# Mixing k and v of six attention pairs with tokens on the partitions

## Chip, cores, metric

One NeuronCore of a Trainium2 chip; the runs did not all use the same chip. The metric is device time in microseconds (us) of one execution. The kernel before takes 245.04 us (median of 6 runs, 244.96 to 245.6).

## The reference

Block-sparse attention whose k and v blocks are first mixed by an 8x8 matrix per head (made by five Sinkhorn steps), then a bilinear feed-forward network (FFN). Four batches, 8 heads, 768 tokens, 64 columns per head; the FFN is 512 to 1536 to 512.

```python
k_sorted = np.einsum('bhij,bhjcd->bhicd', P, k_b)      # block i = sum over blocks j
v_sorted = np.einsum('bhij,bhjcd->bhicd', P, v_b)
scores   = scale * np.matmul(q_b, k_sb.transpose(0, 1, 2, 4, 3))   # within a block of 96 tokens
attn     = softmax(scores)
x        = matmul(attn, v_sb)      # ... heads side by side: 3072 x 512
out      = ((x @ w_a) * (x @ w_b)) @ w_out
```

## The kernel before

Heads are worked in pairs; a batch has four (0 to 15 in all). While the TensorE (PE) runs the FFN of batch b, the attention of batch b+1 is slipped in between its steps as "units": `c_` (mix k and v), `s_` (scores), `o_` (attention output). Tokens are loaded so that partition p holds tokens 6p to 6p+5 (`NCH` = 6). The mix of a pair is 12 matmuls for k and 12 for v. Their stationary operand is a 128-token by 64-column piece of k or v, the moving one the 128x128 mixing matrix `s_all`; the result has head columns on the partitions, so k comes out transposed, as the scores need it, and v is turned back by a DMA transpose.

```python
    def stage_mix(g, what, engines):
        src2 = loaded[g][0 if what == "k" else 1]
        to = (kTs if what == "k" else vTs)[g % NBUF]
        pitch, whole = (BLK, S + PAD) if what == "k" else (P, NB * P)
        mix = psA.tile([P, 2, 512], FP32, tag="A", name="mix")
        for c in range(NCH):
            for e in range(2):
                nc.tensor.matmul(
                    mix[e * D:(e + 1) * D, c // 3, c % 3 * P:(c % 3 + 1) * P],
                    lhsT=src2[:, e, c * D:(c + 1) * D],
                    rhs=s_all[:, 2 * g + e], start=True, stop=True)
        for hf, eng in enumerate(engines):
            n = 2 // len(engines)
            for u in range(n):
                d1 = _ap(to, (hf + u) * 3 * CG, [[whole, P], [CG, 3], [pitch, NB], [1, CG]])
                s1 = _ap(mix, (hf + u) * 512, [[1024, P], [P, 3], [CG, NB], [1, CG]])
                copy(eng, d1, s1)
        if what == "v" and g > HP:
            nc.sync.dma_start_transpose(out=vss[g % NBUF][:, :, V0:V0 + P],
                                        in_=to.rearrange("p i t -> p (i t)"))
# ... cut ...
        def units_full(b):
            g0, us = b * HP, []

            def c_(g):
                if g < 2 * HP - 2:
                    turn_q(g)
                stage_mix(g, "k", ("act",))
                stage_mix(g, "v", ("dve", "act"))
                if 2 * HP - 2 <= g < B * HP - 2:
                    nc.gpsimd.tensor_copy(out=gate, in_=kTs[g % NBUF][0:1, 0:1])
                    load_pair((g + 2) // HP, (g + 2) % HP)

            def s_(g):
                stage_scores(g)
                if g == HP:
                    turn_v(g)
                if g in (HP, HP + 1):
                    stage_q(g + 2)
                if 2 * HP <= g + 1 < B * HP:
                    pair_q(g + 1)
                    stage_q(g + 1)

            def o_(g):
                stage_o(g)
                to_xT(g)

            for u, n in ((c_, 0), (s_, 0), (c_, 1), (s_, 1), (c_, 2), (o_, 0), (s_, 2), (c_, 3),
                         (o_, 1), (s_, 3), (o_, 2), (o_, 3)):
                us.append(lambda u=u, g=g0 + n: u(g))
            return us
# ... cut ...
        def paced(ab, po, units, spare):
            steps = ab + po
            total = len(steps) - 2 * spare
            done = 0
            for now, step in enumerate(steps, 1):
                step()
                while done < len(units) and done * total < now * len(units):
                    units[done]()
                    done += 1
```

An FFN step `ffn_ab` is 8 matmuls with 128x128 weights and 384 moving columns; an output half-step is 6 with 512 columns. Output tiles `o_sb` have three buffers, `hT` has two.

The softmax here doesn't subtract the row's maximum and nothing guards it: scores larger than these inputs give would overflow.

## Time and profile before

| Kernel before | Value | View |
|---|---|---|
| Time | 245.04 us; profiled span 243.3 us | runs, page |
| PE busy | 237.4 us, 98% | page, part 1 |
| Batch 1, batch 2: first FFN matmul to that of the next batch | 54.52 us each, PE busy throughout | windows |
| Batch 3 (no attention inside) to its last matmul | 46.8 us | windows |
| One pair's mix on PE, pauses included | 0.89 us | timeline, worked out below |

The busy table and the slices of the page (40 equal slices of the span, tenths busy; "PEclk" is the granted clock; PE is the TensorE, PEld its weight loads, DVE the VectorE, ACT the ScalarE, POOL the GpSimd, SP the queue of the SyncE):

```profile
PE 237.4 (98%) x2309; PEld 141.6 (58%) x2309; DVE 109.1 (45%) x258; ACT 104.4 (43%) x204; POOL 61.4 (25%) x88
...
PE   7999999999999999999999999999999999999994
...
PEclk9999999999999999999999999999999999999999
DMA  5999999985999589993964369923524310000132
```

PE is the bound from the second slice to the last; the rest has slack. The stages in the windows view (first column start and end, then length, busy us and number of instructions of each engine, granted clock, DMA share, GB/s). The borders come from the chain of work that ended last; they lie 0.17 us behind the first FFN matmul's start in the timeline, in each stage alike, so the lengths are the same:

```profile
84.17:138.69 54.52, 54.52 (x490) 31.41 (x489) 23.57 (x47) 23.89 (x47) 12.67 (x20) 1.00 0.80 124
138.69:193.21 54.52, 54.52 (x490) 31.41 (x489) 23.59 (x47) 23.89 (x47) 7.16 (x11) 1.00 0.54 97
193.21:240.01 46.80, 46.77 (x276) 26.40 (x274) 15.37 (x27) 13.73 (x28) 0.00 (x0) 1.00 0.09 34
```

The Trainium skill, "Perfetto Trace Analysis", section "Tensor Engine Instruction (MATMUL, LD_WEIGHTS)", says that the end of a matmul is estimated by the profiler, not observed, and this trace agrees: a 384-column matmul lasts 326 ns although they start 162.5 ns apart. A pause shorter than that overlap leaves no idle time. So read starts. One mix in batch 1, in the PE timeline (start us, us to the modelled end of the group, group):

```profile
100.55 0.81 PE L332 MATMUL pf<-xT,w_b_sb 128*128 128x384 bf16 x4
101.30 0.53 PE L281 MATMUL mix<-s_all,k 128*64 128x128 bf16 x12
101.66 0.50 PE L281 MATMUL mix<-s_all,v 128*64 128x128 bf16 x12
102.09 0.82 PE L332 MATMUL pf<-xT,w_a_sb 128*128 128x384 bf16 x4
```

The fourth FFN matmul starts at 100.55 + 3 x 0.1625 = 101.04, so its successor could start at 101.20. The first mix matmul starts at 101.30, and the next FFN matmul at 102.09: the mix takes 102.09 - 101.20 = 0.89 us of PE. The weight loads (PEld) of the same stretch show the entry:

```profile
100.39 0.58 PEld L332 LDWEIGHTS <-w_b_sb 128*128 128x128 bf16 x4
101.30 0.36 PEld L281 LDWEIGHTS <-k 128*64 128x64 bf16 x12 [0.32 <-issue]
101.60 0.39 PEld L281 LDWEIGHTS <-v 128*64 128x64 bf16 x12
102.09 0.44 PEld L332 LDWEIGHTS <-w_a_sb 128*128 128x128 bf16 x4
```

A FFN weight load starts while the matmul ahead of it runs (100.39 before 100.55). The first 64-column load does not: it starts with its matmul, at 101.30. ("[0.32 <-issue]" says that the engine stood idle for 0.32 us just before, for nothing that the profile shows.)

### The profile page before, as it was taken

Reading aid. Unit: us, or ns where it says so; the run is one execution under the profiler, and the core shown is the slowest. Engines: PE = TensorE matmul, PEld = TensorE weight load, DVE = VectorE, ACT = ScalarE, POOL = GpSimd, SP = SyncE. Lnnn points to the kernel's source line nnn. Section 1 sums busy time; section 2 is a strip of 40 time slices with the busy share of each in tenths; the row PEclk is TensorE's granted clock in tenths of the full one; section 3 lists DMA queues with packets and bytes.
Section 4 is the critical chain, followed back from the end, with each engine's and each line's share of the span. In section 5 each row is a group of like instructions: output and inputs, shape, how many; then the busy total and the mean of one; then the engine's idle time right before and its main releaser. Section 6 shows DMA issues by size and latency. Waiting matters only on the chain.

```text
span 243.3 us, 5625 instructions
## 1 busy us (share of the span) xinstructions
PE 237.4 (98%) x2309; PEld 141.6 (58%) x2309; DVE 109.1 (45%) x258; ACT 104.4 (43%) x204; POOL 61.4 (25%) x88
## 2 busy tenths in 40 slices
PE   7999999999999999999999999999999999999994
PEld 7776666666554466666654466666654466665442
DVE  6774557555435234464534144363625144344110
ACT  3675853565630175736330165737330133333001
POOL 8766569623220053240400054200000000000000
PEclk9999999999999999999999999999999999999999
DMA  5999999985999589993964369923524310000132
GB/s 78 202 198 196 196 201 201 203 138 83 158 204 153 130 70 155 171 138 70 136 115 122 115 120 114 159 51 58 47 75 131 109 43 0 3 0 1 46 129 86
DMA packets 53930, 28.04 MB, mean 115 GB/s; under 512 B 30736, under 2 KB 50960, under 8 KB 53904
## 3 DMA queue, kind: packets, MB, share of 16 engines
q0 software_dynamic: 20944, 14.16, 41.6%
q1 hardware_dynamic: 32816, 13.45, 28.0%
q8 instruction: 18, 0.29, 0.5%
q14 instruction: 8, 0.07, 0.1%
q10 hardware_dynamic: 144, 0.07, 0.1%
HBM read 28.32 MB, written 6.29 MB: 142 GB/s over the span
## 4 chain that ended last, share of the span: by engine, by line
PE 93%; DVE 4%; ACT 1%; DMA 1%; issue 0%
PE pf L332 52%; PE po L377 24%; PE mix L281 4%; PE o_ps L231 3%; PE sc L302 2%; PE mixh L180 2%; PE po L362 1%; PE vs_ps L208 1%; PE xt_ps L222 1%; PE sc L195 1%; DMA p_nat<-in_sort_net_dram 1%; PE heat L168 1%; PE two L332 1%; PE q_ps L260 1%; DVE xp L237 1%
## 5 line engine op out<-in xcount | busy, mean ns | idle before, releaser
L353 DVE TENSOR_TENSOR hT<-a_sb,pf 128x384 bf16<-128x384 bf16 x95 | 52.6, 553 | 73.8 <-PE pf L332 46.4
L332 PE MATMUL pf<-xT,w_a_sb 128*128 128x384 bf16 x380 | 78.0, 326 | 0.2 <-ACT xT L162 0.2
L332 PE MATMUL pf<-xT,w_b_sb 128*128 128x384 bf16 x380 | 77.5, 326 | 0.0
L352 ACT CAST a_sb<-pf 128x384 bf16<-128x384 f32 x95 | 45.5, 479 | 60.9 <-PE pf L332 41.3
L377 PE MATMUL po<-w_out_sb,hT 128*128 128x512 bf16 x276 | 61.9, 379 | 0.0
L332 PEld LDWEIGHTS <-w_b_sb 128*128 128x128 bf16 x384 | 37.5, 98 | 24.8 <-issue 0.3
L332 PEld LDWEIGHTS <-w_a_sb 128*128 128x128 bf16 x384 | 34.9, 98 | 22.2
L377 PEld LDWEIGHTS <-hT 128*128 128x128 bf16 x276 | 26.3, 98 | 30.0
L162 ACT COPY o_sb<-po 128x512 f32<-128x512 f32 (+1 forms) x13 | 7.5, 577 | 46.8 <-PE po L377 45.2
L164 DVE COPY o_sb<-po 128x512 f32<-128x512 f32 (+1 forms) x12 | 7.9, 656 | 35.2 <-PE po L377 26.3
L307 ACT ACTIVATE eT<-sc 96x768 bf16<-96x768 f32 x24 | 18.0, 802 | 6.9 <-PE sc L302 6.9
L542 POOL COPY gate<-kT 1x1 bf16<-1x1 bf16 x8 | 1.4, 179 | 74.7 <-ACT kT L162 74.7
L237 DVE TENSOR_TENSOR xp<-o_ps,rec 96x512 bf16<-96x512 f32 x24 | 15.9, 684 | 0.6 <-DVE rec L235 0.2
L162 ACT CAST kT<-mix 128x384 bf16<-128x384 f32 x24 | 10.3, 482 | 8.0 <-PE mix L281 8.0
L95 POOL DMA_DIRECT2D k<-in_k_dram x16 | 11.6, 724 | 4.5 <-PE pf L332 2.3
L95 POOL DMA_DIRECT2D v<-in_v_dram x16 | 11.5, 721 | 3.1 <-DMA w_b_sb<-in_moe_w_b_dram 1.2
L231 PEld LDWEIGHTS <-eT 96*128 96x128 bf16 x256 | 10.4, 97 | 3.2 <-DVE xp L237 0.6
L235 DVE RECIPROCAL rec<-o_ps 96x8 f32<-96x8 f32 x32 | 5.6, 189 | 13.8 <-PE o_ps L231 13.8
L231 PE MATMUL o_ps<-vs,eT 96*128 96x65 bf16 x256 | 11.3, 193 | 0.2 <-DVE xp L237 0.2
L246 POOL COPY qc<-q 128x768 bf16<-128x768 bf16 x10 | 8.4, 842 | 7.2 <-DMA q<-in_q_dram 7.2
L95 POOL DMA_DIRECT2D q<-in_q_dram x12 | 8.7, 721 | 1.7 <-DMA w_a_sb<-in_moe_w_a_dram 0.7
L168 PE MATMUL heat<-warm 128*128 128x128 bf16 x84 | 7.6, 264 | 1.3 <-DVE warm L77 1.3
(80 smaller groups left out, 158.3 us busy)
## 6 DMA issues: line engine op xcount, KB each, us to landing
out_dram<-o_sb SPq DMA_DIRECT2D x17, 256.0 KB, 2.0
k<-in_k_dram POOLq DMA_DIRECT2D x16, 192.0 KB, 6.0
v<-in_v_dram POOLq DMA_DIRECT2D x16, 192.0 KB, 6.4
q<-in_q_dram POOLq DMA_DIRECT2D x12, 192.0 KB, 6.7
w_a_sb<-in_moe_w_a_dram POOLq DMA_DIRECT2D x6, 256.0 KB, 9.8
w_b_sb<-in_moe_w_b_dram POOLq DMA_DIRECT2D x6, 256.0 KB, 10.0
w_out_sb<-in_moe_w_out_dram POOLq DMA_DIRECT2D x3, 512.0 KB, 10.8
out_dram<-o_sb SPq DMA_DIRECT2D x12, 128.0 KB, 2.4
```

The costliest lines, as they stand in the source:

```text
L95: nc.gpsimd.dma_start(out=to, in_=_ap(t, base, [[W, P], [S * D, 2], [1, W]]))
L162: nc.scalar.copy(out=out, in_=in_)
L168: nc.tensor.matmul(ps[:, 0:cols], lhsT=warm[:, 0:P], rhs=warm[:, 0:cols], start=True, stop=True)
L231: nc.tensor.matmul(o_ps[:, e, i * (D + 1):(i + 1) * (D + 1)], lhsT=eT[:, hf, e, i * BLK:i * BLK + P], rhs=vs[0:BLK, i0 + i, V0 - 1 + e * ( ...
L237: nc.vector.tensor_tensor(out=_ap(xp, i0 * 2 * D, [[nxp * 2 * D, BLK], [D, 2], [2 * D, NBH], [1, D]]), in0=_ap(o_ps, 1, [[1024, BLK], [511 ...
L246: nc.gpsimd.tensor_copy(out=qc.rearrange("p c e d -> p e c d"), in_=loaded[g][2].rearrange("p e (c d) -> p e c d", c=NCH))
L281: nc.tensor.matmul(mix[e * D:(e + 1) * D, c // 3, c % 3 * P:(c % 3 + 1) * P], lhsT=src2[:, e, c * D:(c + 1) * D], rhs=s_all[:, 2 * g + e], ...
L307: nc.scalar.activation(out=eT[:, hf, :, 0:HB], in_=sc[0:BLK, :, 0:HB], func=AF.Exp, scale=float(scale))
L332: nc.tensor.matmul(pf[:, 0:HW], lhsT=w_sb[:, kc, m * P:(m + 1) * P], rhs=x_cols(b, kc, t), start=(kc == 0), stop=(kc == KA - 1))
L352: nc.scalar.copy(out=a_sb, in_=pf[:, 0:HW])
L353: nc.vector.tensor_mul(out=hT[:, m, t * HW:(t + 1) * HW], in0=a_sb, in1=ab[1][:, 0:HW])
L377: nc.tensor.matmul(held["po"], lhsT=hTs[b][:, m, c * P:(c + 1) * P], rhs=w_out_sb[:, m, :], start=(m == 0), stop=(m == KO - 1))
```

## The change

For pairs 10 to 15 the operands of the mix trade places: `s_all` becomes the stationary operand and a whole head (128 x 384) the moving one, so that the result keeps tokens on the partitions. That makes 4 matmuls per pair out of 24, in the very form of the FFN's. The price is that k is no longer transposed: k and v go through a DMA transpose each, and POOL puts the columns in order (`in_order`), before v is turned back as ever. Since that takes longer, at least two other units stand between each of these mixes and its scores, and batch 2's first two mixes (pairs 12 and 13) are moved into batch 1's steps. The cut of the diff below holds one more move: for pairs 10 to 15 the copy and the DMA transpose of q, which `s_` of the pair before issued, are issued in `c_`, behind the transposes of k and v. Output tiles get six buffers, and `hT` gives one of its two back to make room.

```diff
                 d1 = _ap(to, (hf + u) * 3 * CG, [[whole, P], [CG, 3], [pitch, NB], [1, CG]])
                 s1 = _ap(mix, (hf + u) * 512, [[1024, P], [P, 3], [CG, NB], [1, CG]])
                 copy(eng, d1, s1)
-        if what == "v" and g > HP:
-            nc.sync.dma_start_transpose(out=vss[g % NBUF][:, :, V0:V0 + P],
-                                        in_=to.rearrange("p i t -> p (i t)"))
+
+    def plain(g):
+        return g >= 2 * HP + 2
+
+    def stage_plain(g, what, engines):
+        src2 = loaded[g][0 if what == "k" else 1]
+        mix = psA.tile([P, 2, 512], FP32, tag="A", name="mix")
+        for e in range(2):
+            nc.tensor.matmul(mix[:, e, 0:W], lhsT=s_all[:, 2 * g + e], rhs=src2[:, e],
+                             start=True, stop=True)
+        nat = att.tile([P, NCH, 2, D], BF16, tag="nat", name="nat")
+        step = 2 // len(engines)
+        for u, eng in enumerate(engines):
+            copy(eng, nat[:, :, u * step:(u + 1) * step].rearrange("p c e d -> p e c d"),
+                 mix[:, u * step:(u + 1) * step, 0:W].rearrange("p e (c d) -> p e c d", c=NCH))
+        turned = att.tile([P, NCH, P], BF16, tag="turned", name="turned")
+        nc.sync.dma_start_transpose(out=turned, in_=nat.rearrange("p c e d -> p (c e d)"))
+        st[g, what] = turned
+
+    def stage(g, what, engines):
+        (stage_plain if plain(g) else stage_mix)(g, what, engines)
+
+    def in_order(g, what):
+        if what == "k":
+            to = kTs[g % NBUF][:, 0:S].rearrange("p (i c t) -> p c i t", i=NB, c=NCH)
+        else:
+            to = vTs[g % NBUF][:, :, 0:BLK].rearrange("p i (c t) -> p c i t", c=NCH)
+        nc.gpsimd.tensor_copy(out=to, in_=st[g, what].rearrange("p c (i t) -> p c i t", i=NB))
+
+    def return_v(g):
+        nc.sync.dma_start_transpose(out=vss[g % NBUF][:, :, V0:V0 + P],
+                                    in_=vTs[g % NBUF].rearrange("p i t -> p (i t)"))
 
 
# ... cut: hT bufs=1, o_sb bufs=3 -> bufs=6 in both places ...
-            for u, n in ((c_, 0), (s_, 0), (c_, 1), (s_, 1), (c_, 2), (o_, 0), (s_, 2), (c_, 3),
-                         (o_, 1), (s_, 3), (o_, 2), (o_, 3)):
-                us.append(lambda u=u, g=g0 + n: u(g))
+        plan(0, "c4", "s4", "c5", "s5", "c6", "o4", "s6", "c7", "o5", "s7", "o6", "o7")
+        plan(1, "c8", "s8", "c9", "s9", "c10", "o8", "c11", "o9", "s10", "c12", "s11", "o10", "o11",
+             "c13")
+        plan(2, "s12", "c14", "s13", "o12", "c15", "s14", "o13", "s15", "o14", "o15")
+        after = [[] for _ in seq]
+        for n, (b, u, g) in enumerate(seq):
+            if u is c_ and plain(g):
+                late = 3 if g % HP == 0 else 2
+                after[n + 1] += [lambda g=g, what=what: in_order(g, what) for what in "kv"]
+                if late == 3:
+                    after[n + 3].append(lambda g=g: nc.gpsimd.tensor_copy(
+                        out=gate, in_=xT_of(g // HP - 1)[0:1, HP - 1, 0:1]))
+                after[n + 2 * late - 3].append(lambda g=g: load_later(g))
+                after[n + late].append(lambda g=g: return_v(g))
# ... cut: c_, s_, o_ around stage(); for plain pairs c_ calls pair_q and stage_q behind k and v, which s_ of
# the pair before did; paced() runs batch 1's last unit one step before its end ...
```

More of the change, by code (lines that the diff above doesn't have):

```diff
@@ L336, in hT_of @@
         if b not in hTs:
-            hTs[b] = ffp.tile([P, KO, S], BF16, tag="hT", name="hT")
+            hTs[b] = ffp.tile([P, KO, S], BF16, tag="hT", name="hT", bufs=1)
         return hTs[b]
@@ L363, in ffn_last @@
                                  rhs=w_out_sb[:, m, n0:n1], start=(m == 0), stop=(m == KO - 1))
-            o_sb = ffp.tile([P, 512], FP32, tag="o_sb", name="o_sb", bufs=3)
+            o_sb = ffp.tile([P, 512], FP32, tag="o_sb", name="o_sb", bufs=6)
             copy(eng, o_sb[:, 0:n1 - n0], po[:, 0:n1 - n0])
@@ L384, in store @@
     def store(b, c, po):
-        o_sb = ffp.tile([P, DMODEL], FP32, tag="o_sb", name="o_sb", bufs=3)
+        o_sb = ffp.tile([P, DMODEL], FP32, tag="o_sb", name="o_sb", bufs=6)
         copy("act" if c % 2 == 0 else "dve", o_sb, po)
@@ L531, in units_half, with c_ @@
             return us
-        def units_full(b):
-            g0, us = b * HP, []
-            def c_(g):
-                if g < 2 * HP - 2:
-                    turn_q(g)
-                stage_mix(g, "k", ("act",))
-                stage_mix(g, "v", ("dve", "act"))
-                if 2 * HP - 2 <= g < B * HP - 2:
-                    nc.gpsimd.tensor_copy(out=gate, in_=kTs[g % NBUF][0:1, 0:1])
-                    load_pair((g + 2) // HP, (g + 2) % HP)
-            def s_(g):
-                stage_scores(g)
-                if g == HP:
-                    turn_v(g)
-                if g in (HP, HP + 1):
-                    stage_q(g + 2)
-                if 2 * HP <= g + 1 < B * HP:
-                    pair_q(g + 1)
-                    stage_q(g + 1)
-            def o_(g):
-                stage_o(g)
-                to_xT(g)
-            for u, n in ((c_, 0), (s_, 0), (c_, 1), (s_, 1), (c_, 2), (o_, 0), (s_, 2), (c_, 3),
-                         (o_, 1), (s_, 3), (o_, 2), (o_, 3)):
-                us.append(lambda u=u, g=g0 + n: u(g))
-            return us
+        def c_(g):
+            if g < 2 * HP - 2:
+                turn_q(g)
+            stage(g, "k", ("act",))
+            stage(g, "v", ("dve", "act"))
+            if plain(g):
+                pair_q(g)
+                stage_q(g)
+            else:
+                if g > HP:
+                    return_v(g)
+                if g >= 2 * HP - 2:
+                    nc.gpsimd.tensor_copy(out=gate, in_=kTs[g % NBUF][0:1, 0:1])
+                    load_later(g)
@@ new lines, in s_, with o_, load_later, plan @@
+        def s_(g):
+            stage_scores(g)
+            if g == HP:
+                turn_v(g)
+            if g in (HP, HP + 1):
+                stage_q(g + 2)
+            if 2 * HP <= g + 1 < B * HP and not plain(g + 1):
+                pair_q(g + 1)
+                stage_q(g + 1)
+        def o_(g):
+            stage_o(g)
+            to_xT(g)
+        def load_later(g):
+            if g < B * HP - 2:
+                load_pair((g + 2) // HP, (g + 2) % HP)
+        seq = []
+        def plan(b, *names):
+            for name in names:
+                seq.append((b, {"c": c_, "s": s_, "o": o_}[name[0]], int(name[1:])))
@@ L564, in interleave, with unit @@
+        def unit(u, g, then):
+            u(g)
+            for f in then:
+                f()
+        units = [[] for _ in range(B)]
+        for (b, u, g), then in zip(seq, after):
+            units[b].append(lambda u=u, g=g, then=then: unit(u, g, then))
         def interleave(steps, units, spare, slow=0):
@@ L571, in interleave, with paced @@
                     done += 1
-        def paced(ab, po, units, spare):
+        def paced(ab, po, units, spare, last):
             steps = ab + po
             total = len(steps) - 2 * spare
-            done = 0
+            main, done = len(units) - last, 0
             for now, step in enumerate(steps, 1):
                 step()
-                while done < len(units) and done * total < now * len(units):
+                while done < main and done * total < now * main:
                     units[done]()
                     done += 1
+                if now == len(steps) - 1 and last:
+                    units[main]()
         steps = [lambda: ffn_ab(0, 0, 0, begun[0:2]), lambda: ffn_ab(0, 1, 0, begun[2:4]),
@@ L591 @@
             po = [f for c in range(NCH) for f in ffn_out(b, c)]
-            paced(ab, po, units_full(b + 1) if b + 1 < B else [], 3 if b == 0 else 2)
+            paced(ab, po, units[b], 3 if b == 0 else 2, 1 if b == 1 else 0)
 _INS = ['q', 'k', 'v', 'sort_net', 'moe_w_a', 'moe_w_b', 'moe_w_out']
```

## The prediction

> **What bounds the kernel.** The TensorE stream. The busy table gives it 237.4 of 243.3 us; the timeline shows no gap from 24 us to 240.0 us but 0.18 us at 74.7. In the windows view batches 1 and 2 take 54.52 us each, all PE busy, and batch 3, without attention work, 46.8. DVE (45%), ACT (43%) and POOL (25%) have slack, so only what shortens PE's stream, or makes it wait, moves the time.
>
> **Removed from PE.** A pair's k and v mix is 24 matmuls with 64-column weights and 128 moving columns. In the timeline of batch 1 the last 384-column matmul before a mix starts at 101.04 us (162.5 ns apart: 16 take 2.60 us in the chain), the mix at 101.30 (0.10 us later than that spacing: its narrow weights are not loaded ahead), the next matmul at 102.09. So a mix costs 0.79 + 0.10 = 0.89 us. After: 4 matmuls, 128x128 weights, 384 columns, as the FFN has: 4 x 162.5 ns = 0.65 us, weight loads (98 ns) hidden as they are there. The Trainium skill, "TensorE: Matmul & The Clock Gate", section "Back-to-back issue gap", gives N/2.4 + 2.5 ns = 162.5 ns for 384 columns; the trace agrees. Saving, an estimate: 0.24 us x 6 pairs = 1.4 us. (The old matmuls took only 33 ns each.)
>
> **Added, off the path.** ACT copies k as one 768-wide copy instead of two of 384. Twelve more DMA transposes of 128x768 (like qT's: issue 1.2 us, landing 2.8 to 9.9, median 4.6) and twelve POOL reorders (like the q copy, 0.85 us each) on a nearly idle POOL. An estimate from the stages' DMA shares: 1 us of all DMA engines per transpose, 12 us over 100 us with shares of 0.54 to 0.80: not the bound.
>
> **Does PE wait for them?** From mix to scores now: copies 2 us, transposes landing 4 to 9 us later, two reorders 1.7 us: 8 to 12 us. The schedule leaves 8 to 14 FFN steps of 1.3 us: pairs 10 and 11 about 14 us or more, 12 over 20, 13 (batch 2's second) only 12, 14 17, 15 13. v's second transpose has 9 steps or more. Loads of pairs 12 to 15 now queue on POOL behind the reorders; I estimate 2 to 3 us of margin for 12 and 14. Thin: scores of 13, mixes of 12, 14; expected wait 0.1 us in all. The single hT buffer costs nothing (its last reader is a step before the next writer). Six output buffers remove waits that PE did not feel: batch 3's output copies already wait for PE, not for stores.
>
> **Prediction.** 245.06 - 1.4 + 0.1 = 243.7 us; 8 in 10: 243.3 to 244.9. Faster by over 2%: 0.01; within 2%: 0.96; slower by over 2%: 0.03.
>
> **Signs.** Right: PE instructions about 2189; a mix stretch of 0.65 us in the chain; PE still gapless; batches 1 and 2 shorter by 1.4 us in sum; batch 3 still 46.8. Wrong: PE idle before scores of pairs 10 to 15 (released by POOL), before mixes 12 or 14 (released by loads), or before a batch's first FFN matmul.
>
> **What would make it wrong.** Transposes and loads slowing one another until landing exceeds 10 us (1 to 3 us per late chain); an issue queue blocked behind a transpose that waits for POOL; mix weight loads not hidden (0.1 us each, 2.4 us at worst).

## The result and the profile after

The changed kernel takes 243.53 us (median of 6 runs, 243.25 to 244.04), 1.51 us less than before; the ratio is 0.9935, 95% interval 0.9919 to 0.9951.

```profile
PE 235.4 (97%) x2179; PEld 140.2 (58%) x2189; DVE 109.1 (45%) x258; ACT 104.1 (43%) x198; POOL 70.4 (29%) x97
...
PE   7999999999999999999999999999999999999994
...
PEclk9999999999999999999999999999999999999999
DMA  5999999984999579869994798962315210000132
```

Weight loads fell from 2309 to 2189. (The PE count of 2179 lacks ten records of output matmuls; the trace has 266 of the 276.) POOL has 9 us more, PE is still full in every slice. The same stages, in the windows view:

```profile
84.24:139.59 55.35, 55.19 (x456) 31.75 (x457) 24.51 (x49) 26.25 (x49) 20.20 (x29) 1.00 0.94 146
139.59:191.82 52.23, 52.12 (x400) 29.73 (x401) 22.55 (x45) 21.19 (x39) 8.60 (x11) 1.00 0.61 120
191.82:238.68 46.86, 46.66 (x274) 26.39 (x274) 15.40 (x28) 13.73 (x28) 0.00 (x0) 1.00 0.09 34
```

Batch 1 is longer, because it now holds six mixes, and batch 2 shorter, because it holds two. Their sum is the number to compare: 107.58 us against 109.04, that is 1.46 us less (107.57 and 1.47 from the starts in the timeline, which give the sums below). Batch 3 did not change (46.86 against 46.80). The first mix in the new form, PE and then its weight loads:

```profile
99.34 0.81 PE L361 MATMUL pf<-xT,w_b_sb 128*128 128x384 bf16 x4
99.99 0.49 PE L299 MATMUL mix<-k,s_all 128*128 128x384 bf16 x2
100.32 0.49 PE L299 MATMUL mix<-v,s_all 128*128 128x384 bf16 x2
100.64 0.81 PE L361 MATMUL pf<-xT,w_a_sb 128*128 128x384 bf16 x4
```

```profile
99.34 0.42 PEld L361 LDWEIGHTS <-w_b_sb 128*128 128x128 bf16 x3
99.83 0.58 PEld L299 LDWEIGHTS <-s_all 128*128 128x128 bf16 x4
100.48 0.58 PEld L361 LDWEIGHTS <-w_a_sb 128*128 128x128 bf16 x4
```

The mix starts 0.65 us after the FFN group, with no pause, and takes 0.65 us; both loads run ahead of their matmuls (99.83 before 99.99, 100.48 before 100.64). 0.89 - 0.65 = 0.24 us per mix, 1.4 us for six. A last 0.01 us per mix lies behind it: after an old mix the second FFN matmul starts 173 ns after the first, after a new one 162.5.

The added work stayed off the path. The transposes of `turned` (the tiles that the new DMA transposes write) in the tile view, then the reorders of pair 13 on POOL and the scores that need them on PE:

```profile
DMA to landing us min/median/max: 2.8/4.5/6.3
```

```profile
144.36 0.83 POOL L318 COPY kT<-turned 128x768 bf16<-128x768 bf16 x1 [5.31 <-DMA turned<-nat]
145.12 0.83 POOL L318 COPY vT<-turned 128x768 bf16<-128x768 bf16 x1
```

```profile
149.82 0.52 PE L331 MATMUL sc<-qTf,kT 64*128 64x96 bf16 x16
```

Pair 13 was mixed at 137.48, so its k was ready 7.7 us later (145.2) and 4.6 us before its scores. Over the six pairs of this trace the way from mix to ordered k took 5.1 to 8.6 us, to ordered v 6.4 to 9.8, and the smallest margin before the scores was this one.

### The profile page after: what moved, and what is told of

Its sections match the earlier page's. It is cut to its first block, busy times and chain, and to the rows that moved or that the text cites. A ratio compares the mean times of both kernels' runs of the same rounds, so it can differ in the third digit from the quotient of the medians. Undisturbed runs are those within 1.5% of the kernel's fastest.

```text
span 241.7 us, 5392 instructions
## 1 busy us (share of the span) xinstructions
PE 235.4 (97%) x2179; PEld 140.2 (58%) x2189; DVE 109.1 (45%) x258; ACT 104.1 (43%) x198; POOL 70.4 (29%) x97
## 4 chain that ended last, share of the span: by engine, by line
PE 92%; DVE 4%; ACT 1%; DMA 1%; issue 1%; DVEq 0%
PE pf L361 52%; PE po L406 24%; PE o_ps L231 3%; PE sc L331 2%; PE mix L281 2%; PE mixh L180 2%; PE mix L299 2%; PE po L391 1%; PE vs_ps L208 1%; PE xt_ps L222 1%; PE sc L195 1%; DMA p_nat<-in_sort_net_dram 1%; PE two L361 1%; PE heat L168 1%; PE q_ps L260 1%
## 5 line engine op out<-in xcount | busy, mean ns | idle before, releaser
L406 PE MATMUL po<-w_out_sb,hT 128*128 128x512 bf16 x266 | 61.0, 379 | 0.5
L318 POOL COPY kT<-turned 128x768 bf16<-128x768 bf16 x6 | 5.0, 827 | 35.0 <-DMA turned<-nat 35.0
L574 POOL COPY gate<-kT 1x1 bf16<-1x1 bf16 x4 | 0.7, 178 | 33.3 <-ACT kT L162 33.3
L162 ACT CAST nat<-mix 128x768 bf16<-128x768 f32 (+1 forms) x12 | 7.7, 639 | 4.2 <-PE mix L299 3.5
```

Of the source, the lines that this page charges most:

```text
L162: nc.scalar.copy(out=out, in_=in_)
L406: nc.tensor.matmul(held["po"], lhsT=hTs[b][:, m, c * P:(c + 1) * P], rhs=w_out_sb[:, m, :], start=(m == 0), stop=(m == KO - 1))
```

## The experiments

Eleven kernels ran, all correct. "Sum" is the length of batches 1 and 2 together, from the starts of their FFN matmuls in each trace; it does not depend on how long the start of the program took (which differs, see below). The version with eight pairs is not in the table: it moves mixes into batch 0, so its sum is not comparable; it has its own section.

| Kernel | Sum, us | Time, median us | Ratio to before (95%) |
|---|---|---|---|
| before | 109.04 | 245.04 | 1 |
| changed | 107.57 | 243.53 | 0.9935 (0.9919 to 0.9951) |
| changed, run again | 107.89 | 243.78 | 0.9935 (0.9920 to 0.9950) |
| old mix in the new order | 109.48 | 245.12 | 1.0001 (0.9989 to 1.0013) |
| before with six output buffers | 109.04 | 245.11 | 0.9995 (0.9979 to 1.0011) |
| changed with three output buffers | 107.83 | 243.94 | 0.9950 (0.9935 to 0.9965) |
| new mix, 64-column weights | 108.93 | 244.84 | 0.9988 (0.9976 to 1.0000) |
| new mix, 128-column moves | 108.03 | 244.15 | 0.9953 (0.9939 to 0.9966) |
| batch 2's mixes in place | 117.03 | 252.62 | 1.0305 (1.0274 to 1.0336) |
| reorders three times over | 107.90 | 243.96 | 0.9942 (0.9924 to 0.9960) |
| pair 9's q earlier | 107.56 | 243.77 | 0.9936 (0.9922 to 0.9949) |

The theory: the gain is the PE time of the mix form, and of that nearly all is the pauses where 128-column and 64-column weights follow one another, since the two forms stream equally many columns. (In the kernel before, the 64-column matmuls run two at a time on two halves of the array: in the trace they start 3 ns apart in twos, 56 ns from two to two, so 12 x 56 ns = 0.67 us against 0.65.) Rivals: the number of matmuls; the buffers or the order.

### Old mix in the new order

```diff
     def stage(g, what, engines):
-        (stage_plain if plain(g) else stage_mix)(g, what, engines)
+        stage_mix(g, what, engines)
     def in_order(g, what):
+        if what == "k":   # only the gate that keeps the next load in its place
+            nc.gpsimd.tensor_copy(out=gate, in_=kTs[g % NBUF][0:1, 0:1])
+        return
```

> The changed kernel with the old form of the mix (24 matmuls with 64-column weights per pair) for all pairs, in the new order of units, with the new places of the loads, one hT buffer and six output buffers; no reorders, v is returned as late as in the changed kernel. If the gain is the PE time of the mix form alone, the stages of batch 1 and batch 2 (first FFN matmul to first FFN matmul, less what the two moved mixes shift) sum to 109.0 us as before (107.6 in the changed kernel), PE stays gapless, and the time is that of before: 245.0, 244.7 to 245.4. Rival: the order, the load places or the buffers bring the gain; then 243.5, ratio 0.9935.

Measured 245.12 us, ratio 1.0001. With the old form the gain is gone, though the order, load places and buffers are the new ones. The sum is 0.44 us above that of before, which was not expected; the PE timeline shows one gap there, before the scores of pair 9, on the transpose of pair 9's q:

```profile
97.21 0.51 PE L334 MATMUL sc<-qTf,kT 64*128 64x96 bf16 x16 [0.36 <-DMA qTf<-qc]
```

It is the whole difference: these scores start 1.18 us after the FFN group ahead of them (96.03), and 0.75 us in the kernel before (97.40 to 98.15), 0.43 us more. The idle figure shows 0.36, since the modelled ends cover the rest.

### Before with six output buffers

```diff
-            hTs[b] = ffp.tile([P, KO, S], BF16, tag="hT", name="hT")
+            hTs[b] = ffp.tile([P, KO, S], BF16, tag="hT", name="hT", bufs=1)
-            o_sb = ffp.tile([P, 512], FP32, tag="o_sb", name="o_sb", bufs=3)      # both places
+            o_sb = ffp.tile([P, 512], FP32, tag="o_sb", name="o_sb", bufs=6)
```

> The kernel before with six output buffers and one hT buffer, nothing else. Theory: PE never waited for either, so batches 1 and 2 sum to 109.0 us, time 245.0 to 245.3, ratio 0.999 to 1.001. Rival: the buffers carry part of the gain: below 244.7.

Measured 245.11 us, sum 109.04: nothing. Neither the buffers nor the single `hT` buffer moves the time by itself.

### Changed with three output buffers

```diff
-            o_sb = ffp.tile([P, 512], FP32, tag="o_sb", name="o_sb", bufs=6)      # both places
+            o_sb = ffp.tile([P, 512], FP32, tag="o_sb", name="o_sb", bufs=3)
```

> The changed kernel with three output buffers in place of six. Theory: PE never felt the wait for stores: 243.5, batches 1 and 2 sum to 107.6, no PE gap in the output steps; copies of batch 1 may wait for a store. Rival: with more transposes in the store queue three buffers are too few, PE waits for output copies in batch 1 and part of the gain goes: over 244.

Measured 243.94 us, sum 107.83. PE has no gap in the output steps of batches 1 and 2; the 0.26 us over 107.57 stand at the scores of pair 9 again (0.20 us idle). The interval of its ratio overlaps with that of the changed kernel run again (0.9935 to 0.9965, 0.9920 to 0.9950), so the six buffers are not needed for the gain; an effect below about 0.3 us can't be excluded by the times.

### New mix, 64-column weights

```diff
-            nc.tensor.matmul(mix[:, e, 0:W], lhsT=s_all[:, 2 * g + e], rhs=src2[:, e],
-                             start=True, stop=True)
+            for h in range(2):
+                nc.tensor.matmul(mix[h * PH:(h + 1) * PH, e, 0:W],
+                                 lhsT=s_all[:, 2 * g + e, h * NBH:(h + 1) * NBH],
+                                 rhs=src2[:, e], start=True, stop=True)
```

> The changed kernel with each mix matmul cut in two by output partitions: 8 matmuls per pair with 64-column weights and 384 moving columns, two side by side on the array. Matmul columns streamed are the same as in both kernels. Theory: almost all of the gain is that 64-column weights are not loaded ahead of 128-column matmuls and the other way round, a pause on entry (0.09 to 0.12 us) and on exit (0.10 us) of each mix; both pauses come back, so +0.2 us per pair, +1.2 to 1.3 us in all: 244.7 to 244.9, mix stretch 0.65 us plus pauses, batches 1 and 2 sum to about 108.9. Rival: the gain is from fewer matmuls (24 to 4), by their number: with 8 a fifth of it is lost, 243.8, sum 107.9.

Measured 244.84 us, sum 108.93: the theory's number, not the rival's. The timeline, PE and weight loads:

```profile
99.79 0.81 PE L363 MATMUL pf<-xT,w_b_sb 128*128 128x384 bf16 x4
100.53 0.52 PE L300 MATMUL mix<-k,s_all 128*64 128x384 bf16 x4
100.88 0.49 PE L300 MATMUL mix<-v,s_all 128*64 128x384 bf16 x4
101.30 0.82 PE L363 MATMUL pf<-xT,w_a_sb 128*128 128x384 bf16 x4
```

```profile
100.53 0.47 PEld L300 LDWEIGHTS <-s_all 128*64 128x64 bf16 x8 [0.32 <-issue]
101.30 0.44 PEld L363 LDWEIGHTS <-w_a_sb 128*128 128x128 bf16 x4 [0.30 <-issue]
```

The mix now begins 0.74 us after the FFN group instead of 0.65, and takes 0.77 instead of 0.65: again no load runs ahead where the width changes. 1.36 of the 1.47 us are gone with 64-column weights. That the doubled number of matmuls is not the cause is shown by the next run.

The Trainium skill, "TensorE: Matmul & The Clock Gate", section "Part 3: Packing small matmuls — row/col tiling", lists that a weight load overlaps matmuls in flight only when its row group differs (the text above that list also names a background weight buffer). The traces here differ from the list: 128-row loads overlap 128-row matmuls throughout the FFN steps (99.83 in the changed kernel's weight loads, during the matmul of 99.34's group). In this run and in the kernel before, the overlap stops where the column width changes between 128 and 64. But it is not the column width alone. In the kernel before, the scores' weights have 128 columns and 64 rows, and the attention output's 128 columns and 96 rows:

```profile
98.14 0.37 PEld L302 LDWEIGHTS <-kT 64*128 64x128 bf16 x16 [0.32 <-issue]
105.84 0.69 PEld L231 LDWEIGHTS <-eT 96*128 96x128 bf16 x16
```

The scores start at 98.15, so their load is not ahead, and the entry costs the same 0.10 us (0.75 us after the FFN group at 97.40 instead of 0.65); the attention output starts at 106.00, its load runs 0.16 us ahead, and it has no pause. So a step to weights of half the columns or half the rows shows the pause here, and a step to 96 rows does not. Why, and whether the half width or the two halves side by side count, no run separates.

### New mix, 128-column moves

```diff
-            nc.tensor.matmul(mix[:, e, 0:W], lhsT=s_all[:, 2 * g + e], rhs=src2[:, e],
-                             start=True, stop=True)
+            for u in range(3):
+                nc.tensor.matmul(mix[:, e, u * P:(u + 1) * P], lhsT=s_all[:, 2 * g + e],
+                                 rhs=src2[:, e, u * P:(u + 1) * P], start=True, stop=True)
```

> The changed kernel with each mix matmul cut into three of 128 moving columns: 12 matmuls per pair, each with its own full 128-column weights. Same columns streamed, no narrow weights. Theory: no pause on entry or exit, but a 128-column matmul is shorter than the weight load behind it, as with the transposes of the kernel before (8 in 0.55 us, 69 ns each): mix stretch 0.8 to 0.85 us, +0.15 to 0.2 us per pair, 244.4 to 244.7. Rival: only the width of the weights counts: 0.67 us, 243.6.

My number was wrong and the rival's right. Twelve short matmuls, each with its own full weight load, take 0.67 us:

```profile
100.16 0.50 PE L300 MATMUL mix<-k,s_all 128*128 128x128 bf16 x6
100.50 0.50 PE L300 MATMUL mix<-v,s_all 128*128 128x128 bf16 x6
100.83 0.81 PE L362 MATMUL pf<-xT,w_a_sb 128*128 128x384 bf16 x4
```

They start 56 ns apart. Sum 108.03, of which 0.12 us is the mixes (6 x 0.02) and the rest the wait of pair 9 (0.28 us idle in this trace). The time, 244.15, is 0.4 us above that of the changed kernel run again, which these terms explain only in part; the times of one kernel spread by 0.6 us. Taken with the run above: three times as many matmuls cost 0.02 us per mix, weights of half the width 0.23 (1.36 us over six).

### Batch 2's mixes in place

```diff
-        plan(1, ..., "c11", "o9", "s10", "c12", "s11", "o10", "o11", "c13")
-        plan(2, "s12", "c14", "s13", "o12", "c15", "s14", "o13", "s15", "o14", "o15")
+        plan(1, ..., "c11", "o9", "s10", "s11", "o10", "o11")
+        plan(2, "c12", "s12", "c13", "s13", "c14", "o12", "s14", "c15", "o13", "s15", "o14", "o15")
# reorders right behind the mix where the scores are the next unit
```

> The changed kernel with batch 2's mixes back where the kernel before has them: its first two mixes right before their scores, the reorders right behind the mix. Theory: the new chain from mix to reordered k (copies, two transposes, reorders: 5.1 to 8.6 us in the changed kernel's trace) is longer than the 2 to 3 FFN steps between (2.6 to 3.9 us), so PE stands still 3 to 5 us before the scores of pair 12 and of pair 13, released by POOL, and perhaps up to 2 us before those of pairs 14 and 15: batch 2 grows by 6 to 12 us, time 250 to 256. Rival: DMA and POOL are fast enough in batch 2 and the move was not needed: 243.5 to 244.

Measured 252.62 us, 3.05% slower than before. Batch 2 takes 63.00 us instead of 52.23.

```profile
147.12 0.82 PE L331 MATMUL sc<-qTf,kT 64*128 64x96 bf16 x16 [4.14 <-DMA qTf<-qc]
147.88 1.46 PE L361 MATMUL pf<-xT,w_a_sb 128*128 128x384 bf16 x4
...
159.74 0.52 PE L331 MATMUL sc<-qTf,kT 64*128 64x96 bf16 x16 [2.26 <-DMA qTf<-qc]
160.19 1.46 PE L361 MATMUL pf<-xT,w_a_sb 128*128 128x384 bf16 x4
```

PE stood still 4.14 us and 2.26 us before the scores of pairs 12 and 13. What ended last was not POOL, as I had expected, but the transpose of q, which is third in the store queue behind those of k and v. The waits are 6.4 us. With its four mixes and no wait, batch 2 would take 52.23 + 2 x 0.65 = 53.53 us, so 3.1 us more are missing. The clock explains them: the windows view (last three columns: granted clock, DMA share, GB/s) has two stretches at half clock, one at each gap (the second begins 0.4 us after its gap has ended), and full clock before, between and after.

```profile
146.50:149.91 3.41, 2.79 (x23) 1.67 (x24) 0.00 (x0) 1.98 (x3) 2.80 (x4) 0.50 0.70 95
160.16:163.57 3.41, 3.41 (x16) 1.64 (x12) 0.53 (x1) 1.95 (x3) 1.90 (x3) 0.50 1.04 140
```

PE is busy for 2.79 + 3.41 us in them, half of which, 3.1 us, is lost; four FFN matmuls take 1.46 us instead of 0.81. The Trainium skill, "TensorE: Matmul & The Clock Gate", section "What's actually happening", puts the clock at half rate after an idle window of about 3.4 us; the trace agrees for the first gap, of 4.14 us (slow matmuls start about 320 ns apart instead of 162.5). The gap of 2.26 us was followed by slow ones too, so a gap need not be 3.4 us long by itself.

Most of the waiting here is not that of the new mix itself. The ordered k was there at 144.70 us (143.87 + 0.83 on POOL) and at 157.82; with the usual entry the scores could have started at 142.92 and 157.42. So k alone would have held PE for 1.8 and 0.4 us, and the rest is due to q, whose transpose the change had put behind those of k and v. A version with the mixes in place and q as early as in the kernel before was not run.

### Reorders three times over

```diff
-        nc.gpsimd.tensor_copy(out=to, in_=...)
+        for _ in range(3):
+            nc.gpsimd.tensor_copy(out=to, in_=...)
```

> The changed kernel with each POOL reorder done three times over (same result): POOL +20 us, each chain from mix to reordered k 1.7 us longer, to v and to the next load 3.3 us longer. In the changed kernel's trace k is ready 4.6 us (pair 13) to 14.6 us (pair 12) before its scores. Theory: all of this is off the critical path with room to spare: 243.5, ratio to the kernel before 0.993 to 0.996, PE without new gaps. Rival: POOL copies disturb DVE, or the loads behind them come late, and PE waits: 244.5 or more.

Measured 243.96 us, ratio 0.9942. POOL has 89.9 us busy instead of 70.4, and PE no new gap: only the one before pair 9's scores (0.27 us), where no reorder is concerned. Batch 2, which has four of the six pairs' scores, takes 52.23 us to the hundredth. The reorders are off the path with at least 1.7 us to spare.

### Pair 9's q earlier

The wait for pair 9's q appears in most traces of the new order, and never in the old one. The old order has 12 units over batch 1's steps, the new one 13 and one at the end, so the scores of pair 9 come one FFN step earlier, while the transpose of its q is issued when it always was (us from the start: 91.22 before, 91.01 in the changed kernel run again). Scores of pair 9 before, and in the changed kernel run again:

```profile
98.15 0.52 PE L302 MATMUL sc<-qTf,kT 64*128 64x96 bf16 x16
```

```profile
96.98 0.51 PE L331 MATMUL sc<-qTf,kT 64*128 64x96 bf16 x16 [0.26 <-DMA qTf<-qc]
```

```diff
         def c_(g):
+                if g == 2 * HP:          # before the load of pair 10
+                    pair_q(g + 1)
+                    stage_q(g + 1)
         def s_(g):
-            if 2 * HP <= g + 1 < B * HP and not plain(g + 1):
+            if g + 1 == 2 * HP:
```

> The changed kernel with one move on POOL: pair 9's q copy is issued before the load of pair 10, not behind it, so that its transpose is issued about 3 us earlier. In the traces so far the scores of pair 9 (now one FFN step earlier than in the kernel before) start just when that transpose lands: PE waited 0 us in the changed kernel's trace, 0.20 us in that with three buffers, 0.36 us in that with the old mix. Theory: this is the one wait that the change brought, and what spreads its times (243.25 to 244.04); with it gone, PE has no gap there in any run, times 243.2 to 243.6, median about 243.35. Rival: the spread has another source (the start or the end of the program); then the spread stays and the median is 243.5 to 243.9.

The wait is gone (sum 107.56, no gap), but the transpose came only about 1.1 us earlier relative to the batch, because the store queue was held by the transpose of pair 8's v until 90.4 us. The spread and the median (243.77, 243.28 to 243.99) did not change, so the theory that this wait makes the spread falls; what the trace shows instead is the start of the program: batch 1's first FFN matmul starts at 84.54 us here (times of the chain), 84.24 in the changed kernel and 83.98 to 84.76 in the other traces with the same program up to that point, while batch 0 takes 64.4 us in all of them. The kernel before spreads as much (244.92 to 245.7 in this call). What makes the start vary was not tried.

### Eight pairs in the new form

```diff
     def plain(g):
-        return g >= 2 * HP + 2
+        return g >= 2 * HP
-        plan(0, ..., "o5", "s7", "o6", "o7")
-        plan(1, "c8", "s8", "c9", "s9", "c10", "o8", "c11", "o9", "s10", "c12", "s11", ..., "c13")
+        plan(0, ..., "o5", "s7", "o6", "c8", "o7", "c9")
+        plan(1, "s8", "c10", "s9", "o8", "c11", "s10", "o9", "c12", "s11", "o10", "o11", "c13")
# ... cut: batch 0's last unit, c9, runs one step before its end, as c13 does in batch 1; `late` is 3 for pair 12 alone ...
```

> The changed kernel with the new form for eight pairs instead of six: pairs 8 and 9 too, mixed two units earlier at the end of batch 0's steps. Theory: each pair is worth 0.24 us of PE time wherever it stands: 0.48 us less, 243.0 (242.8 to 243.4), if PE has no new wait; pair 9's q is early here, so its wait is gone as well. Rival: the loads of weights and pairs that fill the DMA engines in batch 0 make the new chain late, PE waits before the scores of pair 8 or 9 and the gain is lost: 243.5 or more.

Measured 243.31 us, ratio 0.9916 (0.9902 to 0.9931). It was run again beside the changed kernel:

> The changed kernel itself, so that it and the eight-pair version stand beside the same runs of the kernel before. Batches 1 and 2 sum to 107.6 us plus whatever the scores of pair 9 wait for their q (0 to 0.4 us); time 243.4 to 243.9, ratio 0.993 to 0.995.

> The version with eight pairs in the new form, on the same chip as the changed kernel. From the first FFN matmul to the first of batch 3 it took 0.8 us less than the changed kernel in the traces (0.48 from two more mixes, the rest from a PE wait of batch 0 that its order of units avoids); theory: time 0.5 to 1.0 us below the changed kernel's median of this call. Rival: the difference was the start of the program only; then the two medians agree to 0.2 us.

Changed again: 243.78 us, 0.9935 (0.9920 to 0.9950). Eight pairs again: 243.23 us (242.85 to 243.56), 0.9912 (0.9895 to 0.9930). From batch 0's first FFN matmul to batch 3's, the changed kernel's two traces take 171.99 and 172.30 us, those with eight pairs 171.18 and 171.47: 0.8 us less both times. Of that, 0.48 is two more mixes; the rest is in batch 0, where the changed kernel's output matmuls of pair 7 stall on their buffer:

```profile
74.16 0.41 PE L231 MATMUL o_ps<-vs,eT 96*128 96x65 bf16 x8
74.75 0.42 PE L231 MATMUL o_ps<-vs,eT 96*128 96x65 bf16 x8 [0.18 <-DVE xp L237]
```

With a mix between the two output units they run in one piece:

```profile
75.03 0.66 PE L231 MATMUL o_ps<-vs,eT 96*128 96x65 bf16 x16
```

This version beats the kernel before, and the changed one by 0.55 us in the medians; the intervals of the two ratios overlap at their ends, so the last step rests on the traces as much as on the times. Pair 9's scores waited 0.23 us for q in the second of its traces, and not in the first: the statement that its q is early there was too strong.

## Why the prediction was right

- **The bound.** PE's stream, as stated. Batch 3 unchanged, the sum of batches 1 and 2 down by 1.47 us against 1.4 predicted, the time 243.53 against 243.7.
- **The size per mix.** 0.89 to 0.65 us was read off two starts in the timeline, and the changed trace shows 0.65. With the 0.01 us behind each mix, six mixes give 1.49 us; 0.015 us of it is lost at pair 9's scores, and 1.47 was measured. The prediction named only the entry pause of 0.10 us and put the rest into the 0.79 us of the mix. The experiments divide it: columns streamed 0.67 against 0.65, pauses about 0.22 (entry 0.09 and a slow first step of 0.02, exit 0.10). The number of matmuls is worth 0.02 us per mix or less, as twelve instead of four showed.
- **Off the path.** Right, with more room than estimated: mix to ordered k and v took 5.1 to 9.8 us, not 8 to 12, and pair 13 had 4.6 us to spare, not almost nothing. Tripled reorders cost nothing.
- **The waits.** Wrong in place, and right in size only by luck. The prediction put 0.1 us of waiting into the scores of pair 13 and the mixes of 12 and 14. None of them waited. The wait is at pair 9, which is mixed in the old form: its scores moved one FFN step ahead, and 0 to 0.3 us of the gain goes there from run to run (sums 107.57 and 107.89). The prediction had checked the distance of every pair with the new form and none of the others.
- **Buffers.** Right: 245.11 with six in the kernel before, 243.94 with three in the changed one.
- **The move of batch 2's mixes** pays nothing by itself (245.12 with the old mix); without it, and with q behind k and v, the new mix costs 9 us, two thirds of it waiting and one third slow clock. Most of that waiting was for q.

## What to carry to other kernels

On a PE that is never idle, look at the starts on either side of a group, not at its busy time: here a change between 128-column and 64-column weights cost about 0.1 us at each edge of a mix and showed as no idle at all, and 64-row weights had the same pause on entry. So try to give small matmuls between large ones the large ones' weight shape. Count the columns streamed, not the matmuls. When work is put into a fixed number of steps, every unit shifts; check the latest input of those that were not changed as well.

## What the Trainium skill lacked or had wrong

- "TensorE: Matmul & The Clock Gate", "Part 3", has weight loads overlap matmuls in flight only when the row group differs. Here full 128-row loads ran ahead of 128-row matmuls all through the FFN steps (0.65 us for four matmuls). What stopped that was a step between full weights and weights of 64 columns (0.09 us on entry, 0.10 us on exit) or of 64 rows (0.10 us on entry). No page gives this cost; "TensorEngine Tiling (Array Packing)", "Key Properties", says that a change of tiling mode drains the TensorE, without a figure.
- The same page, "Back-to-back issue gap", gives about 81 ns per matmul at 128 columns and about 131 ns at 512 as sustained with weight loads. Here the mix's matmuls with 128 moving columns and a full load each started 56 ns apart (12 in 0.67 us), 384-column ones 162.5 ns and 512-column ones 216 ns (36 in 7.77 us), which is the page's formula for the isolated gap.
- The same page speaks of an idle window of about 3.4 us before the clock halves. Here a gap of 2.26 us, too, was followed by 3.41 us at half clock (four matmuls in 1.46 us).
- "DMA: Bandwidth & Descriptors", "DMA Transpose (X-bar)", has no latency for a transpose within on-chip memory. Here one of 128x768 of bf16 took 2.8 to 6.3 us from issue to landing (median 4.5), and each held the issuing queue 1.2 us or more.
